# Fused attention and gated feed-forward: out-projection matmuls spread over all gaps between the score bursts

## The chip, the cores and the metric

The kernel runs on one core of a Trainium2 chip. The metric is the device time of one execution in microseconds (us). Each kernel was executed several times; the time given is the median. One execution was recorded by the hardware profiler, and all rows of the profile come from that one.

The engines are named as in the profile: PE (TensorE, matmuls), PEld (its weight loads), DVE (VectorE), ACT (ScalarE), POOL (GpSimd) and SP (the queue that issues stores and the transposes by DMA). "SPq" and "POOLq" are the queues of those engines.

## The reference

Attention with 16 extra "beacon" keys per head, then a gated feed-forward block on its output:

```python
B, H, S, Nb, D = (8, 8, 576, 16, 64)        # d_model = H*D = 512, d_ff = 1536
k_all = concatenate([beacon_k, k], axis=2); v_all = concatenate([beacon_v, v], axis=2)
scores = q @ k_all.T / sqrt(D)              # causal on the 576 keys, beacons always seen
a = softmax(scores);  x = (a @ v_all)       # -> [B*S, H*D] = [4608, 512]
out = (gelu(x @ w_gate) * (x @ w_val)) @ w_out
```

## The kernel before

All 4608 tokens pass through eight attention stages, one for each batch `b` of 576 tokens. A batch has four pairs of heads (`m` = 0 to 3). After each attention stage follows one chunk of 512 tokens of the gate and value projections (12 tiles `fi`, each of 8 matmuls into one tile `gv_ps`). The out-projection of that chunk (48 matmuls, each 128x128 by 128x512) is not run at once: it is kept as filler and is issued inside the attention stage of the next batch. The ninth chunk has no attention behind it and is run at the end.

The order of all instructions on every engine is the order in which the program issues them (`keep`), so the loop at the end of the kernel is an order written out by hand. Its helpers, for batches 1 to 7:

- `o(n)` issues the next n out-projection matmuls of the chunk before (`out_mms`). They form four groups of 12. Each group sums in one tile `o_ps`, and after its twelfth matmul a copy on DVE (line 349) takes the tile to SBUF, and a store on SP writes it out. Group 0 uses the pool `psum_t`, groups 1 to 3 use `psum_o`. Each of these pools has one buffer.
- `ab(m)` issues scores 0 and 2 of pair m, `cd(m)` scores 1 and 3. One score chunk is a few matmuls into a tile `s_ps`, then one exponential on ACT (line 159) that reads it, then masks on POOL (line 239) on the diagonal blocks of the result. The pool `psum_s` has two buffers, which are also those of `gv_ps`: score 1 can't begin before the exponential of score 0 has ended, score 3 not before that of score 2, and the next pair's scores 0 and 2 not before those of scores 1 and 3.
- `av(m)` issues the value burst: 30 matmuls of exponentials with values into `x_ps` (pool `psum_x`, one buffer), and then `normalize`: four instructions on DVE (lines 287 and 289) which read `x_ps` and write `y_sb`. The burst needs all masks of its pair.
- `turn(b, m)` transposes `y_sb` on PE (line 299) into `y_ps`, again in `psum_t`, and DVE copies it to `xT_sb` (line 300), the input of the gate matmuls.

The first gate tile of a batch takes its matmuls on the fourth pair last (`kk_late`). Behind that tile POOL issues the loads of batch b+2, and SP the transposes by DMA that fill `qkT` for batch b+1. At the start of an attention stage ACT loads the table of the exponential, at its end that of the gelu.

Of the kernel before, what the change touches and what calls it, by code (L numbers as in the profile page):

```python
# [17 lines left out]
NPAIR = H // 2  # L18
# [35 lines left out]
def kernel(  # L54
# [82 lines left out]
    def load_qk(b):  # L137
        q_sb, k_sb = q_ring[b % NRING], k_ring[b % NRING]
        for j in range(4):
            dma(q_sb[:, j, :, :], q[b, :, j * P : (j + 1) * P, :].rearrange("h p d -> p h d"))  # L140
        dma(q_sb[0:64, 4, :, :], q[b, :, 512:576, :].rearrange("h p d -> p h d"))
        load_keys(k, beacon_k, k_sb, b)
# [44 lines left out]
    def warm(b, m, n):  # L187
        w_ps = psum_o.tile([P, D_MODEL], FP32, name="w_ps", tag="o")
        for _ in range(n):
            mm(w_ps, ident, qkT[:, m, 1, 0:512], True, True)  # L190
# [14 lines left out]
    def scores(b, m, c):  # L205
        i = b * NPAIR + m
        if c == 0:
            exp_of[i] = epool.tile([P, 2, EXP_W], BF16, name="expT", tag="expT")
        expT = exp_of[i]
        s_ps = psum_s.tile([P, 2, 512], FP32, name="s_ps", tag="s")  # L210
        for t, s_lo, w, col in CHUNKS[c]:
            for hi in range(2):
                r = slice(64 * hi, 64 * hi + 64)
                mm(
                    s_ps[:, hi, col : col + w],
                    qkT[r, m, 1, t * P : (t + 1) * P],
                    qkT[r, m, 0, NB + s_lo : NB + s_lo + w],
                    True,
                    True,
                )  # L220
        o, w = CHUNK_OFF[c], CHUNK_W[c]
        act(expT[:, :, o : o + w], s_ps[:, :, 0:w], ACT.Exp, scale=QK_SCALE)
        if b:
            masks(b, m, c)

    def masks(b, m, c):
        expT = exp_of[b * NPAIR + m]
        for t, s_lo, _, _ in CHUNKS[c]:
            if s_lo != S_LO[t]:
                continue  # L230
            n = DIAG[t]
            d = expT[0 : KROWS[t], :, EXP_OFF[t] : EXP_OFF[t] + n]
            if b == 0:
                w = tri[0 : KROWS[t], NB : NB + n] if t == 0 else tri[0 : KROWS[t], 0:n]
                w = w.rearrange("p (o n) -> p o n", o=1).to_broadcast([KROWS[t], 2, n])
                keep(nc.vector.tensor_tensor(out=d, in0=d, in1=w, op=ALU.min))  # L236
            else:
                keep(
                    nc.gpsimd.affine_select(  # L239
                        out=d,  # L240
                        in_=d,
                        pattern=[[0, 2], [1, n]],
                        compare_op=ALU.is_ge,
                        fill=0.0,
                        base=NB if t == 0 else 0,
                        channel_multiplier=-1,
                    )
                )
# [5 lines left out]
    def attend(b, m, wide=False):  # L254
        i = b * NPAIR + m
        if wide:
            x_ps = psum_s.tile([P, 1024], FP32, name="xs_ps", tag="s")
        else:
            x_ps = psum_x.tile([P, 1024], FP32, name="x_ps", tag="x")
        expT, v_sb = exp_of.pop(i), v_ring[b % NRING]  # L260
        x_of[i] = x_ps
        for j in range(5):
            for hi in range(2):
                c0 = SLOT[j] + hi * DV
                for t in range(j + 1):
                    e0 = EXP_OFF[t] + Q_LO[j] - S_LO[t]
                    mm(
                        x_ps[:, c0 : c0 + DV],
                        expT[0 : KROWS[t], hi, e0 : e0 + P],
                        v_sb[0 : KROWS[t], t, 2 * m + hi, 0:DV],  # L270
                        t == 0,
                        t == j,
                        skip_group_check=True,
                    )
# [3 lines left out]
    def normalize(b, m):  # L278
        i = b * NPAIR + m
        x_ps = x_of.pop(i)  # L280
        r_sb = npool.tile([P, 10, 1], FP32, name="r_sb", tag="r_sb")
        y_sb = npool.tile([P, 10, D], BF16, name="y_sb", tag="y_sb")
        y_of[i] = y_sb
        for c0, j0, n in ((0, 0, 6), (512, 6, 4)):
            x = x_ps[:, c0 : c0 + n * DV].rearrange("p (j d) -> p j d", d=DV)
            r = r_sb[:, j0 : j0 + n, :]
            keep(nc.vector.reciprocal(r, x[:, :, D:DV]))  # L287
            keep(
                nc.vector.tensor_tensor(  # L289
                    out=y_sb[:, j0 : j0 + n, :], in0=x[:, :, 0:D], in1=r.to_broadcast([P, n, D]), op=ALU.mult  # L290
                )
            )
# [37 lines left out]
    def out_mms(ci, u0, u1, wide=lambda ti: False):  # L330
        for u in range(u0, u1):
            ti, fi = divmod(u, F_TILES)
            if u == 0:
                o_of[ci] = [opool.tile([P, 4, D_MODEL], FP32, name="o_sb", tag="o_sb"), None]
            if fi == 0:
                if wide(ti):
                    o_of[ci][1] = psum_t.tile([P, D_MODEL], FP32, name="o_ps", tag="t")
                else:
                    o_of[ci][1] = psum_o.tile([P, D_MODEL], FP32, name="o_ps", tag="o")
            o_sb, o_ps = o_of[ci]  # L340
            mm(
                o_ps,
                h_of[ci][:, fi, ti * P : (ti + 1) * P],
                wo_sb[:, fi, :],
                fi == 0,
                fi == F_TILES - 1,
            )
            if fi == F_TILES - 1:
                keep(nc.vector.tensor_copy(o_sb[:, ti, :], o_ps))  # L349
                n0 = ci * CH + ti * P  # L350
                keep(nc.sync.dma_start(out=out[n0 : n0 + P, :], in_=o_sb[:, ti, :]))
# [23 lines left out]
    for b in range(B):  # L375
        u = [0]

        def o(n):
            if b:
                out_mms(b - 1, u[0], u[0] + n, lambda ti: ti == 0)  # L380
                u[0] += n

        def ab(m):
            for c in AB:
                scores(b, m, c)

        def cd(m):
            for c in CD:
                scores(b, m, c)

        def av(m, wide=False):
            attend(b, m, wide)
            normalize(b, m)

        keep(nc.scalar.preload_act_table_set(SET_EXP))
        if b == 0:
            for m in range(NPAIR):
                ab(m)
                if m == NPAIR - 1:
                    for mm_ in (0, 1, 2):  # L400
                        for c in AB + CD:
                            if mm_ == 2 or (mm_ == 1 and c in CD):
                                masks(0, mm_, c)
                    av(0)
                    for c in AB:
                        masks(0, m, c)
                else:
                    transpose_pe(0, m + 1, psum_x, "x")
                    if m == 2:
                        for mm_, cs in ((0, AB + CD), (1, AB)):  # L410
                            for c in cs:
                                masks(0, mm_, c)
                cd(m)
                if 1 <= m < NPAIR - 1:
                    warm(b, m, 5)
            for c in CD:
                masks(0, NPAIR - 1, c)
            av(1)
            av(2, wide=True)
            turn(b, 0)  # L420
            turn(b, 1)
            av(3)
            turn(b, 2)
            turn(b, 3)
        else:
            o(6)
            ab(0)
            o(10)
            cd(0)
            o(8)  # L430
            for m in range(1, NPAIR):
                ab(m)
                av(m - 1)
                cd(m)
                o(6 if m < NPAIR - 1 else 5)
                turn(b, m - 1)
            av(3)
            o(7)
            turn(b, 3)
        keep(nc.scalar.preload_act_table_set(SET_GELU))  # L440
        for fi in range(F_TILES):
            gate_val(b, fi, kk_late=fi == 0)
            if b == 0 and 6 <= fi < 10:
                transpose_pe(1, fi - 6, psum_x, "x")
            if fi == 0:
                if b + 2 < B:
                    load_qk(b + 2)
                    load_v(b + 2)
                if NPERM <= b + 1 < B:
                    transpose_dma(b + 1)  # L450
# [34 lines left out]
```

The softmax here doesn't subtract the row's maximum and nothing guards it: scores larger than these inputs give would overflow.

## Time and profile before

| what | value |
|---|---|
| median of 8 runs | 401.08 us (399.91 to 404.08) |
| the profiled execution's own time | 399.95 us |
| its span, first to last instruction | 398.2 us |
| granted clock of TensorE | 1.00 in all slices |
| out-projection matmul, 128x128 by 128x512 | 403 recorded, 380 ns each with its drain |
| value matmul, 128x128 by 128x65 | 930 recorded, 193 ns each with its drain |
| copy of `o_ps` on DVE | 36, 691 ns each |
| the larger multiply of normalize on DVE, and the smaller | 0.56 us, 0.42 us |
| one exponential on ACT, 512 to 1023 ns | 128, 867 ns in the mean |
| table load on ACT | 1.28 us |

A row gives the time from the start of the first instruction of a group, its busy time, the engine, the line, the operation and the tiles (output <- inputs), and in brackets the idle time of the engine ahead of it with what ended it. Matmuls overlap: the busy time of one contains its drain, so a row of n matmuls lasts n pitches plus one drain, and pitches are read from start to start. A few matmul records are missing from the trace. A wait for several things is put down to the one that came last.

### The profile page before, as it was taken

To read this page: it belongs to the slowest core of one execution; us is meant where nothing else is said; L and a number is where in the kernel's file an instruction comes from. 1 tells how busy PE (TensorE), PEld (TensorE's weight loads), DVE (VectorE), ACT (ScalarE), POOL (GpSimd) and SP (SyncE) were. 2 spreads that over 40 slices of the span, in tenths; PEclk is the share of its full clock that TensorE was granted. 3 is DMA by queue.
4 is the path that set the end of the run, shared out by engine and by line. 5 is a ranking of instruction groups with operands and counts; after the bars stand their busy time and mean duration, and the time that the engine had idled before them with its cause. 6 is when DMAs were issued, how large, how long until landed. Compare 5 with 4: busy or idle time off the path is not lost.

```text
span 398.2 us, 7336 instructions
## 1 busy us (share of the span) xinstructions
PE 368.6 (93%) x2960; PEld 186.2 (47%) x3010; DVE 168.1 (42%) x345; ACT 186.2 (47%) x252; POOL 155.0 (39%) x277
## 2 busy tenths in 40 slices
PE   3868998999989998999899999999899989999996
PEld 2454545544454445544554445444544455444442
DVE  1484553544354434433444345333544254333332
ACT  2842247534772377336653575337723673332110
POOL 8722394780359224941487047803300141000000
PEclk9999999999999999999999999999999999999999
DMA  7999997699119950997099914992042010000012
GB/s 90 177 206 204 178 133 91 63 144 149 54 31 153 138 83 34 122 153 85 29 103 135 118 54 53 161 133 64 30 93 53 30 54 26 2 0 28 26 53 105
DMA packets 139153, 36.23 MB, mean 91 GB/s; under 512 B 126832, under 2 KB 134512, under 8 KB 139120
## 3 DMA queue, kind: packets, MB, share of 16 engines
q0 software_dynamic: 103984, 19.14, 65.3%
q1 hardware_dynamic: 35136, 16.62, 20.9%
q8 instruction: 23, 0.38, 0.4%
q14 instruction: 10, 0.08, 0.1%
HBM read 38.27 MB, written 9.44 MB: 120 GB/s over the span
## 4 chain that ended last, share of the span: by engine, by line
PE 81%; ACT 10%; DVE 4%; issue 2%; DMA 1%; POOL 0%; ACTq 0%; POOLq 0%; DVEq 0%
PE gv_ps L156 46%; PE o_ps L156 24%; ACT expT L159 10%; PE s_ps L156 6%; PE y_ps L299 2%; PE x_ps L156 2%; PE t_ps L168 1%; DVE y_sb L289 1%; DVE qkT L179 1%; DMA kb<-in_beacon_k_dram 1%; DVE expT L236 1%; PE w_ps L156 0%; DVE hT_sb L325 0%; ACT ge_sb L159 0%; POOL qk L110 0%
## 5 line engine op out<-in xcount | busy, mean ns | idle before, releaser
L159 ACT ACTIVATE ge_sb<-gv_ps 128x512 bf16<-128x512 f32 x108 | 64.5, 597 | 160.7 <-PE gv_ps L156 160.7
L325 DVE TENSOR_TENSOR hT_sb<-gv_ps,ge_sb 128x512 bf16<-128x512 f32 x108 | 74.7, 692 | 123.4 <-ACT ge_sb L159 123.4
L159 ACT ACTIVATE expT<-s_ps 128x1024 bf16<-128x1024 f32 (+3 forms) x128 | 101.2, 867 | 36.1 <-PE s_ps L156 36.0
L156 PE MATMUL gv_ps<-xT_sb,wv_sb 128*128 128x512 bf16 x430 | 111.9, 379 | 0.1
L156 PE MATMUL gv_ps<-xT_sb,wg_sb 128*128 128x512 bf16 x414 | 109.9, 379 | 1.0
L239 POOL TENSOR_SCALAR_AFFINE_SELECT expT<-expT 128x256 bf16<-128x256 bf16 (+2 forms) x140 | 51.2, 385 | 141.9 <-ACT expT L159 141.9
L156 PE MATMUL o_ps<-wo_sb,hT_sb 128*128 128x512 bf16 x403 | 100.5, 380 | 2.2 <-issue 1.1
L156 PEld LDWEIGHTS <-wv_sb 128*128 128x128 bf16 x432 | 42.3, 98 | 51.0
L156 PEld LDWEIGHTS <-wg_sb 128*128 128x128 bf16 x432 | 41.6, 98 | 48.2
L156 PEld LDWEIGHTS <-hT_sb 128*128 128x128 bf16 x432 | 39.0, 98 | 45.6 <-issue 1.6
L156 PE MATMUL s_ps<-qkT 64*128 64x336 bf16 (+5 forms) x384 | 39.5, 290 | 13.1 <-ACT expT L159 11.3
L349 DVE COPY o_sb<-o_ps 128x512 f32<-128x512 f32 x36 | 24.9, 691 | 46.6 <-PE o_ps L156 44.2
L110 POOL DMA_DIRECT2D v_sb<-in_v_dram x40 | 33.7, 863 | 15.9 <-DMA wv_sb<-in_moe_w_val_dram 3.7
L156 PEld LDWEIGHTS <-expT 128*128 128x128 bf16 (+1 forms) x960 | 31.1, 97 | 9.6 <-POOL expT L239 8.5
L156 PE MATMUL x_ps<-v_sb,expT 128*128 128x65 bf16 x930 | 33.6, 193 | 0.6 <-DVE y_sb L289 0.6
L289 DVE TENSOR_TENSOR y_sb<-x_ps,r_sb 128x384 bf16<-128x384 f32 (+1 forms) x62 | 30.4, 491 | 2.1
L156 PEld LDWEIGHTS <-qkT 64*128 64x128 bf16 x384 | 15.1, 95 | 30.8 <-issue 22.8
L110 POOL DMA_DIRECT2D q_sb<-in_q_dram x30 | 25.3, 859 | 6.1 <-DMA wo_sb<-in_moe_w_out_dram 6.1
L110 POOL DMA_DIRECT2D k_sb<-in_k_dram x30 | 25.4, 897 | 0.2 <-issue 0.2
L300 DVE COPY xT_sb<-y_ps 128x576 bf16<-128x576 bf16 x32 | 14.5, 453 | 19.1 <-PE y_ps L299 19.1
L287 DVE RECIPROCAL r_sb<-x_ps 128x6 f32<-128x6 f32 (+1 forms) x62 | 11.4, 184 | 22.7 <-PE x_ps L156 22.7
L299 PE MATMUL y_ps<-ident,y_sb 128*128 128x128 bf16 (+1 forms) x160 | 14.1, 218 | 3.4 <-DVE xT_sb L300 3.4
(33 smaller groups left out, 90.9 us busy)
## 6 DMA issues: line engine op xcount, KB each, us to landing
out_dram<-o_sb SPq DMA_DIRECT2D x36, 256.0 KB, 2.0
v_sb<-in_v_dram POOLq DMA_DIRECT2D x24, 128.0 KB, 10.3
q_sb<-in_q_dram POOLq DMA_DIRECT2D x24, 128.0 KB, 4.7
k_sb<-in_k_dram POOLq DMA_DIRECT2D x18, 128.0 KB, 7.3
wg_sb<-in_moe_w_gate_dram POOLq DMA_DIRECT2D x3, 512.0 KB, 11.7
wv_sb<-in_moe_w_val_dram POOLq DMA_DIRECT2D x3, 512.0 KB, 13.5
wo_sb<-in_moe_w_out_dram POOLq DMA_DIRECT2D x1, 1536.0 KB, 23.4
v_sb<-in_v_dram POOLq DMA_DIRECT2D x8, 112.0 KB, 9.0
```

The costliest lines, as they stand in the source:

```text
L110: keep(nc.gpsimd.dma_start(out=out_ap, in_=in_ap))
L156: keep(nc.tensor.matmul(out_ap, lhsT, rhs, start=start, stop=stop, **kw))
L159: keep(nc.scalar.activation(out_ap, in_ap, func, **kw))
L168: keep(nc.tensor.transpose(out_ap, in_ap, ident[0:n, 0:n]))
L179: nc.vector.tensor_copy(qkT[:, m, :, NB:SK].rearrange("p w (t r) -> p w t r", r=6), t_ps[:, 0:2, 0:S].rearrange("p w (r t) -> p w t r", r=6),)
L239: nc.gpsimd.affine_select(out=d, in_=d, pattern=[[0, 2], [1, n]], compare_op=ALU.is_ge, fill=0.0, base=NB if t == 0 else 0, channel_multip ...
L287: keep(nc.vector.reciprocal(r, x[:, :, D:DV]))
L289: nc.vector.tensor_tensor(out=y_sb[:, j0 : j0 + n, :], in0=x[:, :, 0:D], in1=r.to_broadcast([P, n, D]), op=ALU.mult)
L299: keep(nc.tensor.transpose(y_ps[:, Q_LO[j] : Q_LO[j] + n], y_sb[0:n, j, :], ident[0:n, 0:n]))
L300: keep(nc.vector.tensor_copy(xT_sb[:, m, b * S : (b + 1) * S], y_ps[:, 0:S]))
L325: nc.vector.tensor_tensor(out=h_of[ci][:, fi, :], in0=gv_ps[:, 1, :], in1=ge_sb, op=ALU.mult)
L349: keep(nc.vector.tensor_copy(o_sb[:, ti, :], o_ps))
```

## The change

Only the loop for batches 1 to 7 changes. The same 48 out-projection matmuls are dealt out otherwise: 17 instead of 24 before pair 1; then, for each of pairs 1 to 3, three, three and four directly behind the value burst, ahead of scores 1 and 3, and four, five and six behind these scores, ahead of the transposes of the pair before; six instead of seven at the end. Nothing else is touched.

```diff
         else:
-            o(6)
+            o(5)
             ab(0)
-            o(10)
+            o(7)
             cd(0)
-            o(8)
+            o(5)
             for m in range(1, NPAIR):
                 ab(m)
                 av(m - 1)
+                o((3, 3, 4)[m - 1])
                 cd(m)
-                o(6 if m < NPAIR - 1 else 5)
+                o((4, 5, 6)[m - 1])
                 turn(b, m - 1)
             av(3)
-            o(7)
+            o(6)
             turn(b, 3)
```

## The prediction

> **What bounds the kernel now.** I read the page first, for the engine that sets the end: engine shares, then the chain that ended last.
>
> ```profile
> span 398.2 us, 7336 instructions
> PE 368.6 (93%) x2960; PEld 186.2 (47%) x3010; DVE 168.1 (42%) x345; ACT 186.2 (47%) x252; POOL 155.0 (39%) x277
> ...
> PE 81%; ACT 10%; DVE 4%; issue 2%; DMA 1%; POOL 0%; ACTq 0%; POOLq 0%; DVEq 0%
> ```
>
> TensorE is the bound, and every matmul of the change exists before and after it. So only TensorE's idle time can be won or lost, and the 10% of the chain on ScalarE says where it is: exponentials that TensorE waits for. The table of waits, for TensorE alone, gives the kind:
>
> ```profile
> PE s_ps L156 <- ACT expT L159: 11.3, 25, 0.9
> ...
> PE y_ps L299 <- DVE xT_sb L300: 3.4, 2, 1.9
> ```
>
> Columns: total us, times, longest. 25 waits, of which 21 are three in each of batches 1 to 7 (the query over one attention stage shows 1.4 in 3). The last row, from batch 0, is kept for later. Then the order in time of one pair (m = 2 of batch 6):
>
> ```profile
> 278.78 0.59 PE L156 MATMUL s_ps<-qkT 64*128 64x512 bf16 x4
> ...
> 279.27 3.13 ACT L159 ACTIVATE expT<-s_ps 128x1024 bf16<-128x1024 f32 x4 [1.14 <-PE s_ps L156]
> ...
> 279.30 1.08 PE L156 MATMUL x_ps<-v_sb,expT 128*128 128x65 bf16 x30
> ...
> 280.35 0.38 PE L156 MATMUL s_ps<-qkT 64*128 64x64 bf16 x6
> ...
> 281.18 0.27 PE L156 MATMUL s_ps<-qkT 64*128 64x208 bf16 x2 [0.45 <-ACT expT L159]
> ...
> 281.38 0.98 PEld L156 LDWEIGHTS <-hT_sb 128*128 128x128 bf16 x6
> ...
> 282.69 0.44 PE L299 MATMUL y_ps<-ident,y_sb 128*128 128x128 bf16 x5
> ...
> 283.06 0.39 PE L156 MATMUL s_ps<-qkT 64*128 64x512 bf16 x2
> ```
>
> Start to start: scores 0 and 2 take 0.52, the value burst 0.92 (30 matmuls, without the drain of the last), a switch to scores 0.09, score 1 0.22, score 3 0.20, six out-projection matmuls 1.30 (0.216 each, from 2.33 for ten with a drain of 0.38), the transposes 0.37. That is 3.62 of a period of 4.28. The missing 0.66 lies around score 3: its PSUM buffer comes free only when the exponential of score 2 ends. Each batch also waits 0.09 before its last transposes. So a batch has 3 x 0.66 + 0.09 = 2.07 us of TensorE idle, seven batches 14.5 us. More than that the change can't bring.
>
> **The change, part by part.** No instruction is added or removed. Of the 48 out-projection matmuls of a batch, 24 stood before pair 1; now 17 do. Three, three and four go between the value burst and score 1; four, five, six instead of six, six, five stand before the transposes; six instead of seven stand before the last ones. Where an accumulation group of 12 ends, its copy (DVE) and its store (SP) move along. I work out the batch from its first out-projection matmul (0) by these lags, each between two rows of batch 6: score 0 to its exponential 0.49; one exponential to the next 0.92, 0.82, 0.85; exponential 0 to score 1 at the earliest 1.08, exponential 2 to score 3 0.99; score 1 to its exponential 0.42; last value matmul to the end of normalize 1.57. Worked on the order before, they give 21.73 from first matmul to the next gate matmul; the trace has 268.09 to 289.82, 21.73 (the record of that first gate matmul is missing; 289.82 is the next one's 290.03 less 0.216).
>
> Pair 0: score 0 moves from 1.40 to 1.18, but its exponential stays at 2.11: the exponential table is loaded until then (268.91 and 1.28). Score 2 waits 0.18 for the buffer of the last gate tile. Exponential 2 starts at 3.03, so score 3 can't start before 4.02, while the seven matmuls end at 3.38 and score 1 at 3.69: idle 0.33. Before, ten matmuls covered both. Together **+0.51**. Pair 1 starts at 5.40 (was 6.41).
>
> Pair 1: value burst 5.91 to 6.83, three matmuls, score 1 at 7.57, score 3 at 7.79, its buffer free at 7.80. **The 0.66 is gone**; four matmuls, transposes; pair 2 starts at 9.23 (3.83 against 4.28, with one matmul more). ScalarE now waits about 0.36 before exponential 1, hidden: the next score pair finds its buffers free by 0.03.
>
> Pair 2: the same with five matmuls; pair 3 starts at 13.28 (4.05). Its value burst needs the mask of score 3 of pair 1 by 10.20 and has it at 10.14.
>
> Pair 3: value burst 13.80 to 14.72, four matmuls to 15.58, score 1 15.67, score 3 to 16.09. Here group 2 ends (5+7+5+3+4+3+5+4 = 36) and the next six open group 3. Both are `o_ps` in psum_o, which has one buffer, so the first of the six waits for the copy out. Before, group 2 ended in front of the transposes, and nearly 3 us lay between. The copy is behind normalize(2) on DVE: 14.69 + 1.57 = 16.26; started 0.09 before that ends, as the following copy does elsewhere, it runs 0.69 and frees the bank, with 0.06 of signal, at 16.92. **+0.83**. Queued behind on TensorE: the six, the transposes of pair 2, value burst 3, the last six, the last transposes and the gate matmuls; none runs ahead, so all of it is on the path.
>
> That a matmul pays for this is where row and rule part. No row of before has an `o_ps` matmul waiting for VectorE: all 403 recorded ones have 2.2 us of idle ahead. By the row alone this costs nothing and the batch would end at 20.57. The Trainium skill, PSUM — Partial Sum Buffer, "Specifications (TRN2)" and "PSUM bank collisions raise a hardware error", speaks against it: eight banks of 512 FP32 per partition, and two engines may not use one bank and quadrant at once. An `o_ps` of 512 f32 is one bank, and the pools take 4 + 1 + 2 + 1 = 8, so no spare exists. I take the rule's side, because the wait of `y_ps` for `xT_sb` in batch 0 is the same kind, and 1.9 at its longest. By the rule the batch ends at 21.35.
>
> End: value burst 3 at 18.54 to 19.46, six matmuls to 20.76, but normalize(3) lets the transposes start at 21.06: **+0.30** where it was 0.09. Gate matmuls at 21.35.
>
> The copies of the other groups end long before their bank's next use. Stores stay on SP ahead of that batch's qkT transposes, as before. POOL's last mask is 0.5 us earlier against the gate stage, so the loads queued behind it are issued 0.5 us earlier too; score 0 comes only 0.22 earlier. In batch 2 the second score pair came 0.25 late (0.83 instead of 0.59 for the four score matmuls; the last qkT transposes there take up to 9.2 us to landing). I take it as hidden now under the idle of pair 0: -0.25 once; if that cover is gone, it comes back.
>
> Sum per batch: -1.98 (three waits) + 0.51 + 0.03 + 0.83 + 0.21 = -0.40, with rounding -0.39; seven batches -2.7, with the -0.25 **-3.0 us**. Batch 0 and the last chunk keep their order. The profiled execution took 399.95 us (span 398.2 plus 1.75 around it) and would take 397.0; it is among the fastest of its runs, whose median is 401.08, so the median goes to **398.1**.
>
> **The rivals.** *The bank wait is hidden.* For it: the row of idle above. Against: one buffer, and DVE works through normalize first. Then the batch ends at 20.57 (0.06 comes back as a wait for a mask), 1.16 less, 8.1 in seven: 392.7.
>
> *The hand-overs slip a little.* Score 3 of pairs 1 and 2 arrives 0.01 before its buffer, score 2 of the next pair 0.03 after, a mask 0.06 ahead of its burst. A slip of 0.1 in each of 21 pairs is 2.1 us. With 0.14 the gain is used up: about 401.
>
> *Slower: ScalarE starves.* Score 1 stands behind three or four more matmuls, so its exponential comes late (7.99 where it could have run at 7.63), then exponential 3, then the buffers of the next pair. If this lag is 0.25 longer than I take it, each pair pays it: 21 x 0.25 = 5.3, less 3.0: 403.3. Measurable slowing starts at 0.24. For it: the margins are all but nil. Against: the lag of 0.42 and the pitches repeat within 0.02 in batch 6, and pair 0 already runs in this order there.
>
> *The change doesn't do what it says*, with the score 3 waits staying: excluded by order alone, since 0.65 of work is put ahead of a wait of 0.66.
>
> **How the numbers follow.** Forecast 0.56; bank hidden 0.09; slip to about nothing 0.21; starved 0.14. The forecast's own range, with hand-overs 0.08 better or worse in each pair, is 396.4 to 399.8. What a measurement of this kernel can tell from no change is about 0.5%, or 2.0 us: 399.1 to 403.1 counts as same. Of the forecast 0.47 lies below 399.1 and 0.09 above; the slip gives 0.04 and 0.17; starved 0.06 of same and 0.08 of slower. So faster 0.60, same 0.32, slower 0.08. The range leaves out most of the hidden bank below and the starved case above: 395.0 to 402.5.
>
> **What would show it.** The row `s_ps` <- ACT falls from 11.3 to about 3 us, and what is left stands in pair 0 of each batch. A new row `o_ps` <- DVE `o_sb`, seven times about 0.8. The wait for `y_sb` before the last transposes grows from 0.09 to about 0.3. The pair that starts after the first lasts 3.8 us, the second 4.05, the batch 42.05 instead of 42.45. ScalarE idles about 0.3 to 0.4 before exponential 1. The prediction is wrong if score 1 or 3 of pairs 1 to 3 waits over 0.1, if a value burst waits for POOL, or if the bank wait isn't near 0.8.

## The result and the profile after

The changed kernel takes 397.26 us in the median of 11 runs (396.71 to 398.45), the kernel before 400.59 us in 32 runs. The ratio of the mean times is 0.9912, with a 95% interval of 0.9891 to 0.9933, which is 2.7 to 4.4 us less; the medians differ by 3.3 us. Forecast were 398.1 us and 3.0 us less, with a range of 395.0 to 402.5; the time lies in it. The profiled execution of the changed kernel took 398.20 us, among the longest of its runs; that of before, with 399.95, was among the shortest of its own. So the two spans, 398.2 and 396.5, show only 1.7 of the gain, and the comparison has to be made by stage.

The page of the changed kernel, engine shares of the chain that ended last and the row of the out-projection:

```profile
PE 78%; DVE 9%; ACT 6%; issue 3%; DMA 2%; POOL 1%; POOLq 0%; DVEq 0%
...
L156 PE MATMUL o_ps<-wo_sb,hT_sb 128*128 128x512 bf16 x402 | 101.8, 379 | 7.0 <-DVE o_sb L349 5.3
```

ScalarE's share of the chain fell from 10% to 6%, VectorE's rose from 4% to 9%: one wait was exchanged for another. The idle time ahead of the `o_ps` matmuls was 2.2 us, none of it put down to another engine; now it is 7.0, and for 5.3 of it VectorE's copy is named. The waits of TensorE alone say the same (total us, times, longest):

```profile
PE o_ps L156 <- DVE o_sb L349: 5.3, 7, 0.8
...
PE s_ps L156 <- ACT expT L159: 1.7, 3, 0.9
```

The waits of scores for exponentials fell from 11.3 us in 25 to 1.7 in 3, and the same query over batch 0 shows that these three are all there, where nothing was changed. Seven waits for the copy of `o_ps` are new, one in each of batches 1 to 7.

The length of a batch can be read in the chain that ended last, in order of time, from the first gate matmuls of one batch to those of the next. Before:

```profile
120.22 10.74 PE gv_ps L156 x49
...
162.68 2.32 PE gv_ps L156 x10
```

and after:

```profile
120.49 8.42 PE gv_ps L156 x39
...
162.52 2.59 PE gv_ps L156 x12
```

42.46 became 42.03. Read from last transposes to last transposes, which is how all batch times below are read, batches 3 to 7 took 42.44 to 42.46 before and 42.02 to 42.04 after, 0.42 less. Batch 2 took 42.70 before and 42.03 after, batch 1 0.27 less. From the end of batch 0 to that of batch 7 the two profiles differ by 301.11 - 298.06 = 3.05 us. What hides it in the spans is batch 0, which has the same instructions in both: it ended at 31.09 in the one execution and at 32.36 in the other.

The order in time of pairs 1 to 3 of batch 6, after, TensorE and VectorE (start, length, engine):

```profile
272.55 0.59 PE L156 MATMUL s_ps<-qkT 64*128 64x512 bf16 x4
...
273.07 1.09 PE L156 MATMUL x_ps<-v_sb,expT 128*128 128x65 bf16 x30
...
274.74 0.48 PE L156 MATMUL s_ps<-qkT 64*128 64x64 bf16 x8
...
276.40 0.59 PE L156 MATMUL s_ps<-qkT 64*128 64x512 bf16 x4
...
280.46 0.58 PE L156 MATMUL s_ps<-qkT 64*128 64x512 bf16 x4
...
282.12 0.81 PE L156 MATMUL o_ps<-wo_sb,hT_sb 128*128 128x512 bf16 x3
...
282.86 0.47 PE L156 MATMUL s_ps<-qkT 64*128 64x64 bf16 x8
...
283.01 0.42 DVE L289 TENSOR_TENSOR y_sb<-x_ps,r_sb 128x256 bf16<-128x256 f32 x1
...
283.35 0.68 DVE L349 COPY o_sb<-o_ps 128x512 f32<-128x512 f32 x1
284.09 1.46 PE L156 MATMUL o_ps<-wo_sb,hT_sb 128*128 128x512 bf16 x6 [0.76 <-DVE o_sb L349]
...
288.16 0.45 PE L299 MATMUL y_ps<-ident,y_sb 128*128 128x128 bf16 x5
```

Scores 1 and 3 now stand in one row of eight matmuls: no wait splits them as in the kernel before. Pair 1 lasts 3.85 (272.55 to 276.40; worked out: 3.83), pair 2 4.06 (4.05). In pair 3 the matmuls of group 2 end at 282.93 (the first of the four is missing from the row), but their copy starts only at 283.35, just before the last multiply of normalize ends at 283.43. The copy ends at 284.03, and the six matmuls of group 3 begin 0.06 later.

### The profile page after: what moved, and what is told of

Read it like the earlier page. It is cut to its first block, busy times and chain, and to the rows that moved or that the text cites. A ratio compares the mean times of both kernels' runs of the same rounds, so it can differ in the third digit from the quotient of the medians.

```text
span 396.5 us, 7336 instructions
## 1 busy us (share of the span) xinstructions
PE 369.3 (93%) x2960; PEld 183.1 (46%) x3010; DVE 167.2 (42%) x345; ACT 188.0 (47%) x252; POOL 155.0 (39%) x277
## 4 chain that ended last, share of the span: by engine, by line
PE 78%; DVE 9%; ACT 6%; issue 3%; DMA 2%; POOL 1%; POOLq 0%; DVEq 0%
PE gv_ps L156 46%; PE o_ps L156 16%; PE x_ps L156 8%; PE s_ps L156 5%; DVE y_sb L289 4%; ACT expT L159 3%; PE y_ps L299 2%; DMA qk<-in_k_dram 2%; ACT L395 2%; ACT ge_sb L159 1%; DVE r_sb L287 1%; DVE o_sb L349 1%; PE t_ps L168 1%; POOL qk L110 1%; DVE expT L236 1%
## 5 line engine op out<-in xcount | busy, mean ns | idle before, releaser
L159 ACT ACTIVATE expT<-s_ps 128x1024 bf16<-128x1024 f32 (+3 forms) x128 | 103.0, 861 | 27.6 <-PE s_ps L156 25.4
L156 PE MATMUL gv_ps<-xT_sb,wg_sb 128*128 128x512 bf16 x421 | 111.5, 379 | 1.0
L156 PE MATMUL gv_ps<-xT_sb,wv_sb 128*128 128x512 bf16 x424 | 110.4, 379 | 0.0
L156 PE MATMUL o_ps<-wo_sb,hT_sb 128*128 128x512 bf16 x402 | 101.8, 379 | 7.0 <-DVE o_sb L349 5.3
L156 PEld LDWEIGHTS <-hT_sb 128*128 128x128 bf16 x432 | 38.0, 97 | 45.8 <-issue 6.6
L156 PE MATMUL s_ps<-qkT 64*128 64x336 bf16 (+5 forms) x384 | 38.6, 293 | 4.2 <-ACT expT L159 1.7
L156 PEld LDWEIGHTS <-qkT 64*128 64x128 bf16 x384 | 14.1, 95 | 30.6 <-issue 22.5
```

Source lines behind the costliest of these rows:

```text
L156: keep(nc.tensor.matmul(out_ap, lhsT, rhs, start=start, stop=stop, **kw))
L159: keep(nc.scalar.activation(out_ap, in_ap, func, **kw))
```

## The experiments

All deals are written as in the change: matmuls ahead of pair 1 / behind the value bursts / ahead of the transposes / at the end. Before is 6, 10, 8 / 0, 0, 0 / 6, 6, 5 / 7; the change is 5, 7, 5 / 3, 3, 4 / 4, 5, 6 / 6. The theory under test is the prediction's: one serial order on TensorE, into which each wait comes with its own length, whatever is gained elsewhere. The rivals stand in the expectations. The ratios to the kernel before, with their 95% intervals, are formed from all runs and not from the medians, so they differ a little from the quotient of two medians.

| kernel | batch, expected | batch, measured | time, expected | median, measured |
|---|---|---|---|---|
| the change | 42.05 | 42.03 | 398.1 | 397.26 |
| e1, normalize behind the copy | 41.65 | 41.65 | 394.5 | 394.66 |
| e2, bank wait covered | 41.9 | 42.00 | 396.4 | 396.70 |
| e3, split alone | 41.79 | 41.89 | 396.0 | 397.02 |
| e4, front alone | 42.97 | 42.95 | 404.2 | 403.38 |
| e5, dealt anew | 41.28 | 41.34 | 392.4 | 393.03 |
| e6, more ahead | 43.07 | 43.07 | 405.0 | 404.56 |
| e7, seven at the end | 41.82 | 41.81 | 395.8 | 396.02 |
| e8, before again | 42.45 | 42.45 | - | 400.61 (one run) |

### e1: normalize behind the copy

```diff
                 ab(m)
-                av(m - 1)
+                attend(b, m - 1)
+                if m < NPAIR - 1:
+                    normalize(b, m - 1)
                 o((3, 3, 4)[m - 1])
+                if m == NPAIR - 1:
+                    normalize(b, m - 1)
                 cd(m)
```

> In pair 3 alone, normalize(2) is issued on DVE behind the copy of o_ps instead of ahead of it; TensorE's order is that of the changed kernel. If the bank wait is a copy that stands behind normalize on DVE, the copy starts 0.4 us earlier, the wait falls from 0.76 to about 0.4, and the batch lasts 41.65 us instead of 42.03: about 394.5 us in all against 397.3 (2.7 less). If the wait lies beside ScalarE's work and is free (the rival that the bank costs nothing), time and batch stay at 397.3 and 42.03. If delaying normalize makes the transposes of pair 2 late, a wait for y_sb appears ahead of them and eats the gain; by the lags it should be under 0.05.

394.66 us, a ratio to before of 0.9837 (0.9778 to 0.9897). VectorE's order in time in pair 3 of batch 6:

```profile
280.06 0.69 DVE L349 COPY o_sb<-o_ps 128x512 f32<-128x512 f32 x1 [1.95 <-PE o_ps L156]
280.67 0.18 DVE L287 RECIPROCAL r_sb<-x_ps 128x6 f32<-128x6 f32 x1
```

and TensorE's:

```profile
280.80 1.46 PE L156 MATMUL o_ps<-wo_sb,hT_sb 128*128 128x512 bf16 x6 [0.38 <-DVE o_sb L349]
```

The wait is halved, to 0.38, and the batch is shorter by just that: 0.38. So the wait was in full on the path that sets the end, and half of it was the queue on VectorE, the rest the copy itself. The rival that the bank costs nothing falls. Normalize, now later, does hold up a weight load of the transposes of pair 2, by 0.28 in this batch, but these transposes start at 282.10, right behind the six matmuls: that costs nothing, as expected.

### e2: the bank wait covered

Deal 5, 7, 5 / 3, 3, 3 / 4, 9, 3 / 6:

```diff
-                o((3, 3, 4)[m - 1])
+                o((3, 3, 3)[m - 1])
                 cd(m)
-                o((4, 5, 6)[m - 1])
+                o((4, 9, 3)[m - 1])
```

> Four matmuls moved from pair 3 to pair 2 (behind the value bursts 3, 3, 3; ahead of the transposes 4, 9, 3), so that group 2 ends in front of the transposes of pair 1 and the copy has pair 3 to itself. The row o_ps <- DVE must vanish (7 waits, 5.3 us). If that wait were all, the batch would fall by 0.8 to 41.25 us and the time to about 391.7. By the lags, the wait has been covering another: with three matmuls behind scores 1 and 3 of pair 3 its last value burst comes about 0.7 us ahead of its masks on POOL, and the batch is 41.9, the time about 396.4.

396.70 us, 0.9889 (0.9818 to 0.9959), and a batch of 42.00: nothing to speak of came of taking the wait away. TensorE's waits no longer have the `o_ps` row; in its place stands

```profile
PE x_ps L156 <- POOL expT L239: 3.0, 14, 0.3
```

and the last value burst of batch 6, in order of time, shows where:

```profile
283.76 0.39 PE L156 MATMUL x_ps<-v_sb,expT 128*128 128x65 bf16 x7 [0.18 <-POOL expT L239]
...
284.39 0.63 PE L156 MATMUL x_ps<-v_sb,expT 128*128 128x65 bf16 x15 [0.25 <-POOL expT L239]
```

The burst is broken in three by masks that aren't there yet. From its first matmul to the next out-projection matmul it takes 1.69 (283.17 to 284.86), where the burst of pair 2 takes 0.92 (280.16 to 281.08): the masks cost 0.77, as much as the bank wait had cost. The chain from scores 1 and 3 over the exponentials to the masks needs some 2.5 us in which TensorE must have other work (in the changed kernel, scores 1 and 3 of pair 3 start at 282.86 and the last mask ends at 285.37); the six matmuls and their wait in the changed kernel had given it that. Taking away the one wait alone let the other come out, as expected; but the 0.13 per batch that were expected to remain (42.03 less 41.9) were 0.10 too much.

### e3: the split alone

Deal 6, 10, 8 / 3, 3, 3 / 3, 3, 2 / 7, the kernel before with part of each gap's matmuls moved ahead of scores 1 and 3:

```diff
                 av(m - 1)
+                o((3, 3, 3)[m - 1])
                 cd(m)
-                o(6 if m < NPAIR - 1 else 5)
+                o((3, 3, 2)[m - 1])
```

> Only the split of the gaps: 6, 10, 8 ahead of pair 1 and seven at the end as in the kernel before, three behind each value burst, and 3, 3, 2 ahead of the transposes in place of 6, 6, 5. Groups end under cover. The 0.66 in front of score 3 must vanish in all three pairs (2.0 per batch). By the lags most of it does not come in: with fewer matmuls ahead of the transposes, score 2 of pairs 2 and 3 waits 0.18 for its buffer and the last value burst 0.9 for its mask, so the batch is 41.79 us and the time about 396.0, 4.6 less than before. If the split as such were worth the whole wait, the batch would be 40.5 and the time 386.9.

397.02 us, 0.9893 (0.9858 to 0.9929), and a batch of 41.89. The waits for exponentials in pairs 1 to 3 are gone, worth 1.98 per batch; only 0.56 comes in. The row

```profile
PE x_ps L156 <- POOL expT L239: 4.4, 14, 0.4
```

is again the last burst waiting for masks. In batch 6, in order of time:

```profile
281.38 0.78 PE L156 MATMUL s_ps<-qkT 64*128 64x512 bf16 x4
...
284.89 0.41 PE L156 MATMUL x_ps<-v_sb,expT 128*128 128x65 bf16 x8
...
286.79 1.68 PE L156 MATMUL o_ps<-wo_sb,hT_sb 128*128 128x512 bf16 x7
```

The last burst takes 1.90 to the next out-projection matmul, where 0.93 is usual: 0.97 more (expected: 0.9). Scores 0 and 2 of pairs 2 and 3 last 0.78 each instead of 0.58, for their buffer: 0.20 more in each (expected: 0.18). Together that is 1.37 of the 1.42 that don't come in. So the split alone is worth less than the wait that it removes. Even so its batch is 0.14 shorter than that of the changed kernel: what the change does beside splitting the gaps costs more than it brings. One batch of this execution, batch 2, took 42.82; it is spoken of below.

### e4: the front alone

Deal 5, 7, 5 / 0, 0, 0 / 7, 12, 5 / 7, as edits of the changed kernel (two lines between the parts are left out):

```diff
-                o((3, 3, 4)[m - 1])
+                o((0, 0, 0)[m - 1])
                 cd(m)
-                o((4, 5, 6)[m - 1])
+                o((7, 12, 5)[m - 1])
...
-            o(6)
+            o(7)
```

> Only the front of the change: 5, 7, 5 ahead of pair 1, nothing behind the value bursts, 7, 12, 5 ahead of the transposes, seven at the end (groups end under cover). The waits of score 3 in pairs 1 to 3 stay (0.66 each) and pair 0 gets its idle of 0.51: batch 42.97 us, 404.2 in all, 3.6 more than before. The rival that the gain comes from starting pair 1 earlier (ScalarE's exponentials begin 1 us sooner) expects less than 400.6.

403.38 us, slower, 1.0058 (1.0021 to 1.0096), and a batch of 42.95: 0.50 more than before, where 0.51 was worked out for pair 0. The waits of scores for exponentials are all still there:

```profile
PE s_ps L156 <- ACT expT L159: 11.2, 25, 0.9
```

So starting pair 1 earlier is a loss by itself.

### e5: dealt anew

Deal 6, 10, 8 / 3, 2, 1 / 3, 4, 4 / 7, as an edit of the kernel before:

```diff
+                o((3, 2, 1)[m - 1])
                 cd(m)
-                o(6 if m < NPAIR - 1 else 5)
+                o((3, 4, 4)[m - 1])
```

> The deal that the same lags give as best: 6, 10, 8 before pair 1 (as in the kernel before), behind the value bursts 3, 2, 1, ahead of the transposes 3, 4, 4, seven at the end. Groups end in front of cover (24 and 36). Expected: no bank wait, no idle in pair 0, score 3 waits of about 0, 0.05 and 0.45, a buffer wait of 0.2 in pair 2, a mask wait of 0.1 in pair 3, 0.09 at the end: batch 41.28 us, 392.4 us in all, 8.2 less than before. As pair 0 has no idle time now, the late transposes by DMA of batch 2 are uncovered again: that batch may be 0.25 longer than the rest. The rival (what counts is that every gap has matmuls, also those of pair 0 by fewer ahead) expects it between the two kernels, at 397 to 400.

393.03 us, 0.9808 (0.9741 to 0.9875): it beats both kernels, the changed one by 4.2 us and by 0.69 per batch. What TensorE still waits for in one attention stage is, by the wait rows, a single one:

```profile
PE s_ps L156 <- ACT expT L159: 0.3, 1, 0.3
```

Shorter gaps stand in no row of waits, but in the lengths: in batch 6 scores 0 and 2 of pair 2 last 0.78 instead of 0.58 (expected: a wait of 0.2), and the last value burst 1.26 instead of 1.09 (expected: a wait of 0.1). Batch 2 is as long as the others (41.34), against the expectation that it might be 0.25 longer.

### e6: more ahead

Deal 5, 7, 5 / 6, 6, 4 / 1, 2, 6 / 6:

```diff
-                o((3, 3, 4)[m - 1])
+                o((6, 6, 4)[m - 1])
                 cd(m)
-                o((4, 5, 6)[m - 1])
+                o((1, 2, 6)[m - 1])
```

> The changed kernel with six matmuls behind the value bursts of pairs 1 and 2 in place of three, and 1, 2, 6 ahead of the transposes: ScalarE gets scores 1 and 3 0.65 us later. By the lags it then idles about 1 us in front of exponential 1, and scores 0 and 2 of the next pair wait 0.4 to 0.6 for their buffers: batch 43.07 us, 405.0 in all, 1.0 per batch above the changed kernel. This is the slower rival of the prediction, brought about on purpose. If ScalarE has slack there (the rival that TensorE's order in a gap doesn't matter as long as it has work), the batch stays at 42.03 and the time at 397.3.

404.56 us, 1.0087 (1.0043 to 1.0132), a batch of 43.07: 1.04 above the changed kernel. TensorE's waits have both kinds now:

```profile
PE s_ps L156 <- ACT expT L159: 5.7, 18, 0.9
PE o_ps L156 <- DVE o_sb L349: 5.3, 7, 0.8
```

Three more matmuls ahead of scores 1 and 3 in two pairs turn the gain into a loss. ScalarE has no slack there; the slower rival of the prediction can be brought about, with the price that the lags gave it.

### e7: seven at the end

Deal 5, 7, 5 / 3, 3, 4 / 4, 5, 5 / 7:

```diff
-                o((4, 5, 6)[m - 1])
+                o((4, 5, 5)[m - 1])
                 turn(b, m - 1)
             av(3)
-            o(6)
+            o(7)
```

> One matmul of pair 3 moved back to the end: 4, 5, 5 ahead of the transposes and seven in front of the last ones. The wait for y_sb ahead of the last transposes is normalize(3) less the matmuls put into it, so it falls from 0.30 to 0.09, the bank wait stays at 0.76: batch 41.82 us, 395.8 in all. If the last transposes wait for something else, the batch stays at 42.03.

396.02 us, 0.9869 (0.9823 to 0.9915), a batch of 41.81: 0.22 less than with six, one matmul's length. TensorE's weight loads wait for `y_sb`, in the changed kernel and here:

```profile
PEld L299 <- DVE y_sb L289: 5.8, 8, 1.3
...
PEld L299 <- DVE y_sb L289: 4.3, 8, 1.3
```

4.3 is what they waited before, too, and seven times 0.22 is 1.5. So the last transposes do wait for normalize(3), and a seventh matmul fits into that wait at no cost.

### e8: the kernel before, again

No edit.

> The kernel before, unchanged, profiled once more. Tells what of a profile repeats: the batches should again be 42.44 to 42.46 us. If the 0.25 by which batch 2 was longer (late transposes by DMA) is of the kernel, batch 2 is again about 42.7; if it is of that execution, it is about 42.45. The end of batch 0 (31.09 us after the span's start in the first profile) may differ by about 1 us, with the first loads.

Batches of 42.44 to 42.46, batch 2 with 42.45 among them. Batch 0 ended at 31.97. So the 0.25 by which batch 2 was longer belongs to the first execution and not to the kernel.

## Why the prediction was right, point by point

**The waits of score 3** (-1.98 per batch): right. The waits are gone in pairs 1 to 3, and pairs 1 and 2 last what was worked out, to 0.02.

**Pair 0** (+0.51): right, 0.50 alone in e4. Scores 0 and 2 of pair 0 of batch 6, then its scores 1 and 3, before:

```profile
269.49 0.58 PE L156 MATMUL s_ps<-qkT 64*128 64x512 bf16 x4
...
272.27 0.47 PE L156 MATMUL s_ps<-qkT 64*128 64x64 bf16 x8
```

and after:

```profile
268.33 0.77 PE L156 MATMUL s_ps<-qkT 64*128 64x512 bf16 x4
...
270.65 0.79 PE L156 MATMUL s_ps<-qkT 64*128 64x64 bf16 x8
```

They last 0.19 and 0.32 longer, where 0.18 and 0.33 were worked out. Only the sign to watch for was named wrongly: this idle time doesn't stand as a wait for ScalarE in TensorE's waits, as the prediction said it would (some 3 us of that row).

**The bank wait** (+0.83): right in kind, place and size. The row of before and the page cited in the prediction had parted here: before, no `o_ps` matmul waited for VectorE, and by that row alone the forecast would have been 392.7 us. Now seven do, and in batch 6 the six matmuls begin 0.06 after the copy ends. What the runs show is that the next group waits until the copy has emptied the one buffer; that two engines may not use one bank and quadrant at once (the Trainium skill, PSUM — Partial Sum Buffer, "PSUM bank collisions raise a hardware error") no run here tests. The row's 0.76 counts from the end of the drain of the scores, the prediction's 0.83 from the last score's pitch. Counted its way, scores 1 and 3 start 15.71 and the six matmuls 16.94 after the batch's first out-projection matmul, at 267.15; worked out were 15.67 and 16.92, so the wait is 0.81. e1 shows that it is paid in full.

**The end** (+0.30 instead of 0.09): right, by e7.

**Sum per batch**: -0.39 worked out, -0.42 measured. The difference lies behind the bank wait: the last transposes of batch 6 start 21.01 after its first out-projection matmul, and 21.06 was worked out. Batch 1 gained only 0.27, because it had less to lose: before, its pairs last 4.21 to 4.22 and not 4.28, as the waits ahead of score 3 are shorter there; why, stays open.

**The -0.25 for the late transposes by DMA**: this step failed. It treated something that one execution showed as the kernel's own. e8 and e5 have no idle time in pair 0 that could hide late transposes, and batch 2 isn't longer in them. Such a delay does occur: e3 had one in batch 2, seen in its order of time,

```profile
101.53 0.37 PE L156 MATMUL s_ps<-qkT 64*128 64x464 bf16 x2 [0.74 <-DMA qkT<-q_sb]
```

and that batch took 0.93 more. Why it came late there stays open. Whether idle time in pair 0 covers such a delay, as the prediction held, was seen only once and small: e7, with the front of the change, has one such wait of 0.2 in batch 6, and that batch is no longer than the others. Without this term the forecast would have been 2.7 us less. What repeats in the profiles is six batches of 0.42 and one of 0.27, 2.8 us; the medians say 3.3, with an interval from 2.7 to 4.4, and the runs don't tell where the rest comes from. So it is luck that the 3.0 lies nearer to 3.3 than 2.7 does. Of the 0.8 by which 398.1 lies above 397.26, 0.5 comes from the starting point: it was reckoned from a median of 401.08 us in eight runs, and 32 runs have 400.59.

**The rivals**: the hidden bank is ruled out by e1. The slips did not occur: the pairs last within 0.02 of what the lags gave. ScalarE does idle ahead of exponential 1, 0.26 in pairs 1 and 2 of batch 6 (forecast 0.3 to 0.4), but that stays hidden in the changed kernel. Starved further it costs time: e6 prices that at 1.04 us per batch for three matmuls more in each of two pairs.

## What to carry to other kernels

Where one engine sets the end and the rest is order, write its order out by lags from the trace: for the changed kernel and seven variants the batch came out within 0.1 us of what the lags gave. Before moving filler into a gap, look at three things: whose buffer the first moved instruction needs and which queue frees it, what the gap that it left had covered, and what the next chain (here exponentials, then masks) still needs as cover. In this kernel, a group that ends in front of transposes has its copy covered; one that ends in front of the next group in the same buffer pays for it. And a forecast of several terms is worth checking term by term: parts of the change cost time (the front 0.50, the end 0.22), and the deal of e5, worked out from the same lags, gains more than twice as much as the change.

## What was not expected

Ten profiles show batch 0, with the same instructions in all, ending between 30.57 and 32.45 us after the span's start, 1.9 us apart; that is more than half of the gain, so spans of single profiles can't be compared here. Batch times can: batches 3 to 7 repeat within 0.03 us in each profile. And a wait that was removed in full (5.3 us in e2) gave back even less than was expected, 0.03 us per batch, 0.2 in seven, because it had been the cover of another.
